# An mLSTM cell followed by hash-routed experts: unread products on TensorE between the two stages, and a shorter hand-over

## The chip, the cores and the metric

The kernel runs on one core of a Trainium2 chip. The metric is the device time of one execution in microseconds (us), taken as the median of several runs. The other numbers come from a profile of one execution: for every engine the instructions with start and duration, and the clock that TensorE was granted over time. The engines are called as in the profile: PE (TensorE, matmuls, with PEld for its weight loads), DVE (VectorE), ACT (ScalarE), POOL (GpSimd) and SP (the queue that issues most transfers).

## The reference, cut to what matters

Two stages follow each other. The first is a recurrent attention cell over 4 batches, 8 heads, 768 steps and heads of 40; its result is laid out as 3072 rows of 320 values. The second sends each row to one of 8 experts by a hash of its token, and each expert is two matrix products with a relu between them.

```python
# stage 1 (per step t): gates, then
C = f_stab * C + i_stab * einsum('bhd,bhe->bhde', vt, kt)
n = f_stab * n + i_stab * kt
h_tilde = einsum('bhde,bhe->bhd', C, qt)
denom = maximum(abs(einsum('bhd,bhd->bh', n, qt)), 1.0)
y[:, :, t] = sigmoid(o_gate[:, :, t]) * h_tilde / denom
# bridge: (B,H,S,D) -> (B*S, H*D)
x = attn_out.transpose(0, 2, 1, 3).reshape(3072, 320)
# stage 2
expert_idx = token_ids * 2654435761 % 8
for e in range(8):
    mask = expert_idx == e
    h = maximum(x[mask] @ w1[e], 0.0)      # 320 -> 1024
    out[mask] = h @ w2[e]                  # 1024 -> 320
```

Everything is fp32 at the inputs and outputs.

## The kernel before

Stage 1 runs over NT = 24 tiles of 128 rows. The last step of each tile, `finish`, divides by the denominator and stores the 128 rows to a scratch array `x_d` in device memory. The two halves of that step are a product on DVE out of PSUM and a product on POOL.

```python
def finish(s):
    ...
    nc.vector.tensor_tensor(den[:], den[:], hs[:, :, :, D:D1], op=ALU.max)
    x = wk.tile([P, H, D], F32, name="x")
    xv = x.rearrange("p (j f) d -> p f j d", f=2)
    nc.vector.tensor_tensor(                                       # L436
        xv, hs[:, :, :, :D], og[s].rearrange(...), op=ALU.mult)
    nc.vector.reciprocal(den[:], den[:])                           # L439
    nc.gpsimd.tensor_tensor(xv, xv, den[:].to_broadcast(...), op=ALU.mult)   # L440
    return lambda: nc.sync.dma_start(x_d[s * P : (s + 1) * P, :], ...)       # L441
```

Stage 2 cannot start before all 24 stores have landed, because an expert's rows may come from any tile. For each expert it gathers NJ = 3 tiles of 128 rows by index, and for each group of EG = 4 experts one further tile with RM = 32 remaining rows of each of them. A gathered tile is turned on PE (three 128x128 transposes into one PSUM tile `tp`) and copied to `xT`, so that an expert works on CAP = 3 * 128 + 32 = 416 columns.

```python
def turn(xg, dst, on_act):
    tp = mps.tile([P, DB, P], F32, name="tp")
    for db in range(2):
        nc.tensor.transpose(tp[:, db, :], xg[:, db * P : (db + 1) * P], ident[:])   # L810
    nc.vector.tensor_copy(xg[:, Dm:], xg[:, 2 * P : Dm])                            # L811
    nc.tensor.transpose(tp[:, 2, :], xg[:, 2 * P :], ident[:])                      # L812
    if on_act:
        nc.scalar.copy(dst, tp[:])                                                  # L814
    else:
        nc.vector.tensor_copy(dst, tp[:])                                           # L816

def turns(e):
    xT = xTs[e] = xp.tile([P, DB, CAP], F32, name="xT")
    def tile_of(j):
        turn(xgs[e][:, j, :], xT[:, :, j * P : (j + 1) * P], j % 2 == 1)
    def remainder():
        i = e % EG
        if i == 0:
            remT[e // EG] = xp.tile([P, DB, P], F32, name="remT")
            turn(xgs[-1 - e // EG], remT[e // EG][:], True)
        nc.gpsimd.tensor_copy(xT[:, :, NM:], remT[e // EG][:, :, i * RM : (i + 1) * RM])   # L896
    return [lambda j=j: tile_of(j) for j in range(NJ)] + [remainder]
```

The driver fetches for two experts, turns the tiles of expert 0, and then goes through the experts. While expert e computes, the tiles of expert e + 1 are turned between its products.

```python
fetch(0)                     # four gathers on POOL: three tiles, then the remainders of four experts
fetch(1)
third = weight_slices(2)
for piece in turns(0):       # the three tiles and the remainder of expert 0
    piece()
for e in range(E):
    ...
    layer1(W[e], xTs[e], h, CAP, one)   # mh[128 x 416] <- w1, xT   (L827, L834)
    ...
    layer2(W[e], h, NJ, ...)            # zp[128 x 320] <- h, w2    (L863)
```

The PSUM tiles of stage 2 come from one pool: `tp` and `zp` with two buffers each, `mh` with four. The weights of experts 0 and 1 are loaded during stage 1.

Of the kernel before, what the change touches and what calls it, by code (L numbers as in the profile page):

```python
# [8 lines left out]
F32 = mybir.dt.float32  # L9
# [5 lines left out]
ALU = mybir.AluOpType  # L15
PSUM = bass.MemoryType.PSUM

P = 128
# [4 lines left out]
def kernel(  # L23
# [24 lines left out]
    nc = tc.nc  # L48
    B, H, S, D = q.shape
# [4 lines left out]
    E, _, F = moe_w1.shape  # L54
    FB = F // P
    NT = N // P
    PR = H // 2
# [9 lines left out]
    RM = 32  # L67
    EG = P // RM
    NM = NJ * P
    CAP = NM + RM  # L70
# [11 lines left out]
    ident = consts.tile([P, P], F32, name="ident")  # L82
# [4 lines left out]
    def weights(src1, src2, wpool, w2pool):  # L87

        w1t = wpool.tile([P, 2, F], F32, name="w1t")
        w1c = wpool.tile([P, FB // 2, P], F32, name="w1c")  # L90
        w2t = w2pool.tile([P, FB, Dm], F32, name="w2t")
        s1 = src1[: 2 * P, :].rearrange("(a p) f -> p a f", p=P)
        last = src1[2 * P :, :].rearrange("d (a two f) -> two d a f", two=2, f=P)
        s2 = src2.rearrange("(a p) d -> p a d", p=P)
        parts = [
            (t[:, db, f0 : f0 + F // 2], s1[:, db, f0 : f0 + F // 2])
            for t in (w1t,) for db in range(2) for f0 in (0, F // 2)
        ]
        parts += [(w1c[i * P // 2 : (i + 1) * P // 2], last[i]) for i in range(2)]
        parts += [(w2t[:, fb : fb + 2, :], s2[:, fb : fb + 2, :]) for fb in range(0, FB, 2)]  # L100
        return (w1t, w1c, w2t), [lambda eng=nc.sync, d=d, r=r: eng.dma_start(d, r) for d, r in parts]

    W = {}

    def weight_slices(e):

        W[e], slices = weights(moe_w1[e], moe_w2[e], wpools[e % 3 // 2], w2pools[2 <= e < 6])
        return slices
# [8 lines left out]
    with tc.tile_pool(name="gates", bufs=1) as gp, \  # L117
# [308 lines left out]
        def finish(s):  # L426
            d = st.pop(s)
            hs = d["xo"].rearrange("p f i (x d) -> p f (i x) d", d=DP)
            den = wk.tile([P, 2, PR, 1], F32, name="den")
            nc.vector.tensor_scalar(  # L430
                den[:], hs[:, :, :, D:D1], scalar1=-1.0, scalar2=1.0, op0=ALU.mult, op1=ALU.max,
# [5 lines that stand above are left out]
                xv, hs[:, :, :, :D], og[s].rearrange("p (j f) d -> p f j d", f=2), op=ALU.mult,  # L437
            )
            nc.vector.reciprocal(den[:], den[:])  # L439
            nc.gpsimd.tensor_tensor(xv, xv, den[:].to_broadcast([P, 2, PR, D]), op=ALU.mult)  # L440
            return lambda: nc.sync.dma_start(x_d[s * P : (s + 1) * P, :], x.rearrange("p h d -> p (h d)"))  # L441


# [343 lines left out]
    mps = ctx.enter_context(tc.tile_pool(name="mps", bufs=2, space=PSUM))  # L787

    def gather(xg, idx):
        nc.gpsimd.indirect_dma_start(  # L790
            out=xg, out_offset=None, in_=x_d[:, :], in_offset=bass.IndirectOffsetOnAxis(ap=idx, axis=0),
        )
# [13 lines left out]
# [8 lines that stand above are left out]
            nc.scalar.copy(dst, tp[:])  # L814
        else:
            nc.vector.tensor_copy(dst, tp[:])  # L816

    def layer1(w, xT, h, cols, between=lambda fp: None):

        w1t, w1c, _ = w  # L820
        for fp in range(FB // 2):
            hp = [mps.tile([P, CAP], F32, name="mh", bufs=4) for _ in range(2)]

            def halves(first):
                for i in range(2):
                    r = slice(i * P // 2, (i + 1) * P // 2)
                    nc.tensor.matmul(  # L827
                        hp[i][:, :cols], lhsT=w1c[r, fp, :], rhs=xT[r, 2, :cols], start=first, stop=not first,
                    )

            def whole(i, first):
                fb = 2 * fp + i
                for db in range(2):
                    nc.tensor.matmul(  # L834
                        hp[i][:, :cols], lhsT=w1t[:, db, fb * P : (fb + 1) * P], rhs=xT[:, db, :cols],
                        start=(first and db == 0), stop=(not first and db == 1),
                    )

            def out(i):
                if i == 0:  # L840
                    nc.vector.tensor_relu(h[:, 2 * fp, :cols], hp[i][:, :cols])  # L841
                else:
                    nc.scalar.activation(h[:, 2 * fp + 1, :cols], hp[i][:, :cols], AF.Relu)  # L843

            if fp % 2 == 0:
                for i in range(2):
                    whole(i, True)
                between(fp)
                halves(False)
                for i in range(2):  # L850
                    out(i)
            else:
                halves(True)
                for i in range(2):
                    whole(i, False)
                    out(i)
                between(fp)
# [15 lines left out]
    with tc.manual_schedule():  # L873
        xgs, xTs, remT, hrem = {}, {}, {}, {}

        def fetch(e):
            if e % EG == 0:
                xgs[-1 - e // EG] = xp.tile([P, DB * P], F32, name="xr")
            xgs[e] = xp.tile([P, NJ, DB * P], F32, name="xg", bufs=3)
            for j in range(NJ):  # L880
                gather(xgs[e][:, j, :Dm], cols_of(g_idx, e * NJ)(j))
            if e % EG == 0:
                gather(xgs[-1 - e // EG][:, :Dm], cols_of(g_idx, NR + e // EG)(0))
# [8 lines that stand above are left out]
                i = e % EG  # L892
                if i == 0:
                    remT[e // EG] = xp.tile([P, DB, P], F32, name="remT")
                    turn(xgs[-1 - e // EG], remT[e // EG][:], True)
                nc.gpsimd.tensor_copy(xT[:, :, NM:], remT[e // EG][:, :, i * RM : (i + 1) * RM])  # L896

            return [lambda j=j: tile_of(j) for j in range(NJ)] + [remainder]

        def rest(g):  # L900
            zp = mps.tile([P, Dm], F32, name="zp")
            for fb in range(FB):
                for i in range(EG):
                    nc.tensor.matmul(
                        zp[i * RM : (i + 1) * RM, :], lhsT=hrem[g][:, i, fb, :], rhs=W[g * EG + i][2][:, fb, :],
                        start=(fb == 0), stop=(fb == FB - 1),
                    )
            scatter(zp, cols_of(s_idx, NR + g)(0), True)

        fetch(0)  # L910
        fetch(1)

        third = weight_slices(2)
        for piece in turns(0):
            piece()
        for e in range(E):
            g, i = e // EG, e % EG
            if e + 2 < E:
                fetch(e + 2)
            h = xp.tile([P, FB, CAP], F32, name="h")  # L920
            if i == 0:
                hrem[g] = xp.tile([P, EG, FB, RM], F32, name="hrem")
            ahead = turns(e + 1) if e + 1 < E else []

            def one(_):
                if ahead:
                    ahead.pop(0)()
                for _ in range(3):
                    if third:
                        third.pop(0)(nc.scalar)  # L930

            def after(j):
                one(j)
                if j == 0 and i == EG - 1:
                    rest(g)

            layer1(W[e], xTs[e], h, CAP, one)
            nc.gpsimd.tensor_copy(hrem[g][:, i], h[:, :, NM:])  # L938
            layer2(W[e], h, NJ, cols_of(s_idx, e * NJ), True, after)
            if e + 3 < E:  # L940
                load_weights(e + 3)

    nx = nc.values_load(xe[0:1, NX : NX + 1], min_val=0, max_val=NX)
    with tc.If(nx > 0):
        with tc.For_i(0, nx, 1) as k:
# [11 lines left out]
            xT = xp.tile([P, DB, CAP], F32, name="xT")  # L957
# [35 lines left out]
```

## Time and profile before

| | before |
|---|---|
| median of 3 runs | 429.63 us (429.09 to 429.99) |
| span of the profiled execution | 427.9 us |
| PE busy | 386.1 us (90% of the span) |
| DVE, ACT, POOL busy | 136.1, 134.6, 118.7 us |
| first transposes of stage 2 start | 173.34 us |
| first expert product starts | 179.17 us |

A row of the profile names the source line, the engine, the operation and its tiles, as output <- inputs. One fp32 matmul of the source appears as two PE records, one fp32 transpose as one. The chain of work is the sequence that ended last, followed back from the end: each piece waited for the one before it. A table of stretches gives for every stretch the busy time of each engine, then PEclk, the clock granted to PE as a share of full speed, and last the share of the transfer engines and their GB/s.

### The profile page before, as it was taken

The page shows a single profiled execution, that of the slowest core. Times are in us where ns is not written, and L with a number is a line of the kernel's source. Part 1 is how long each engine was busy: PE and PEld are TensorE (multiplying, and loading weights), DVE is VectorE, ACT ScalarE, POOL GpSimd, SP SyncE. Part 2 cuts the span into 40 slices and gives each one's busy share as a digit, 9 for nine tenths or more (in the row PEclk, how much of TensorE's full clock was granted, in tenths as well). Part 3 has the DMA queues.
Part 4 walks back from the last instruction along what each step waited for, and adds up shares of the span by engine and source line. Part 5 has one row for each costly group of instructions (what it writes and reads, how often), then busy time and mean ns, then how long its engine had stood idle before and what let it go on. Part 6 is the DMA issues. An engine that isn't in the chain of part 4 may idle for free.

```text
span 427.9 us, 7402 instructions
## 1 busy us (share of the span) xinstructions
PE 386.1 (90%) x2862; PEld 258.5 (60%) x2862; DVE 136.1 (32%) x371; ACT 134.6 (31%) x238; POOL 118.7 (28%) x204
## 2 busy tenths in 40 slices
PE   2369999999999992599999999999999999999992
PEld 2257867877887871356656557556556566575551
DVE  7464748766675761211020120110110210201100
ACT  5158776686495471011010110110111111111010
POOL 6363323313323422710321501302302312021021
PEclk9868999999999998589999999999999999999997
DMA  8929998899676720527616318235216201000000
GB/s 168 213 61 172 206 218 180 190 205 214 149 161 129 161 90 33 163 96 239 193 46 212 120 29 271 62 98 170 75 64 214 61 8 38 0 15 31 1 17 30
DMA packets 111784, 51.37 MB, mean 120 GB/s; under 512 B 86624, under 2 KB 105892, under 8 KB 111748
## 3 DMA queue, kind: packets, MB, share of 16 engines
q1 hardware_dynamic: 105898, 39.31, 38.2%
q0 software_dynamic: 2496, 8.20, 6.0%
q10 hardware_dynamic: 3354, 3.37, 2.4%
q8 instruction: 23, 0.38, 0.4%
q14 instruction: 13, 0.11, 0.1%
HBM read 42.00 MB, written 8.63 MB: 118 GB/s over the span
## 4 chain that ended last, share of the span: by engine, by line
PE 78%; issue 5%; ACT 5%; DMA 4%; POOL 2%; DVE 1%; SPq 1%; ACTq 0%; POOLq 0%; DVEq 0%
PE mh L834 22%; PE zp L863 21%; PE mh L827 6%; PE sp L351 6%; PE ht L409 6%; PE ht L402 3%; PE ab L311 2%; PE tr L275 2%; PE xo L424 2%; PE ht L382 2%; PE tk L588 1%; PE tp L810 1%; ACT qT L289 1%; PE xb L323 1%; PE tr L288 1%
## 5 line engine op out<-in xcount | busy, mean ns | idle before, releaser
L863 PE MATMUL zp<-w2t,h 128*128 128x320 f32 x384 | 105.2, 433 | 0.0
L834 PE MATMUL mh<-xT,w1t 128*128 128x416 f32 x256 | 98.9, 531 | 0.9 <-POOL xT L896 0.9
L863 PEld LDWEIGHTS zp<-w2t,h 128*128 128x128 f32 x384 | 72.7, 190 | 32.1 <-issue 3.3
L834 PEld LDWEIGHTS mh<-xT,w1t 128*128 128x128 f32 x256 | 47.8, 194 | 44.0 <-issue 41.6
L816 DVE COPY xT<-tp 128x384 f32<-128x384 f32 x16 | 8.9, 558 | 142.3 <-PE tp L812 124.7
L797 POOL DMA_INDIRECT out_dram<-zo,s_idx x26 | 25.6, 986 | 92.5 <-ACT zo L796 92.5
L843 ACT ACTIVATE h<-mh 128x416 f32<-128x416 f32 x32 | 16.6, 517 | 110.1 <-PE mh L827 60.3
L796 ACT COPY zo<-zp 128x320 f32<-128x320 f32 x26 | 11.1, 426 | 101.1 <-PE zp L863 92.9
L841 DVE TENSOR_SCALAR h<-mh 128x416 f32<-128x416 f32 x32 | 18.9, 592 | 53.4 <-PE mh L834 26.9
L359 DVE TENSOR_TENSOR w<-sp,w 128x512 f32<-128x512 f32 x48 | 30.9, 686 | 13.8 <-PE sp L351 10.3
L440 POOL TENSOR_TENSOR x<-x,den 128x320 f32<-128x320 f32 x24 | 17.4, 724 | 64.0 <-DVE den L439 34.1
L351 PE MATMUL sp<-qT,kT 64*128 64x128 f32 x384 | 29.7, 297 | 4.1 <-ACT qT L289 4.1
L351 PEld LDWEIGHTS sp<-qT,kT 64*128 64x128 f32 x384 | 24.9, 199 | 10.8 <-ACT qT L289 6.0
L315 ACT ACTIVATE w<-ab 128x512 f32<-128x512 f32 x48 | 26.6, 611 | 5.0 <-PE ab L311 4.9
L409 PE MATMUL ht<-w,v 128*64 128x128 f32 x384 | 27.1, 285 | 0.0
L827 PE MATMUL mh<-xT,w1c 64*128 64x416 f32 x128 | 26.7, 535 | 0.0
L938 POOL COPY hrem<-h 128x256 f32<-128x256 f32 x8 | 3.2, 400 | 84.1 <-ACT h L843 84.1
L790 POOL DMA_INDIRECT xg<-x_rows,g_idx x24 | 23.4, 976 | 9.7 <-issue 9.7
L417 ACT COPY hT<-ht 128x512 f32<-128x512 f32 x24 | 14.1, 587 | 31.2 <-PE ht L409 31.2
L409 PEld LDWEIGHTS ht<-w,v 128*64 128x64 f32 x384 | 21.2, 140 | 4.0 <-issue 3.1
L289 ACT COPY qT<-tr 128x512 f32<-128x512 f32 x24 | 22.9, 975 | 0.6 <-PE tr L288 0.3
L275 PE MATMUL tr<-ident,k 128*128 128x128 f32 x96 | 17.2, 307 | 4.3 <-DMA k<-in_k_dram 4.3
(177 smaller groups left out, 407.0 us busy)
## 6 DMA issues: line engine op xcount, KB each, us to landing
w2t<-in_moe_w_dram SPq DMA_DIRECT2D x28, 320.0 KB
w1t<-in_moe_w_dram SPq DMA_DIRECT2D x28, 256.0 KB
k<-in_k_dram SPq DMA_DIRECT2D x24, 160.0 KB
v<-in_v_dram SPq DMA_DIRECT2D x24, 160.0 KB
og<-in_o_gate_dram SPq DMA_DIRECT2D x24, 160.0 KB
x_rows<-x SPq DMA_DIRECT2D x24, 160.0 KB
ql<-in_q_dram SPq DMA_DIRECT2D x6, 480.0 KB
w1c<-in_moe_w_dram SPq DMA_DIRECT2D x14, 128.0 KB
```

Source lines behind the costliest of these rows:

```text
L275: nc.tensor.transpose(tp[:, j, :], d["k"][:, 2 * j : 2 * j + 2, :].rearrange("p h d -> p (h d)"), ident[:])
L289: nc.scalar.copy(qb[b]["T"][:, :, cols], tp[:])
L315: nc.scalar.activation(w[:, hf], ab[:], AF.Exp)
L351: nc.tensor.matmul(sp[hf][:, j, :], lhsT=d["kT"][r, j, :], rhs=q_of(s)[r, j, :], start=True, stop=True,)
L359: nc.vector.tensor_tensor(d["w"][:, hf], d["sp"][hf][:], d["w"][:, hf], op=ALU.mult)
L409: nc.tensor.matmul(place(j, hf), lhsT=d["v"][:, 2 * j + hf, :], rhs=d["w"][:, hf, j, :], start=(c == 0 and j0 == 0), stop=True, skip_group ...
L790: nc.gpsimd.indirect_dma_start(out=xg, out_offset=None, in_=x_d[:, :], in_offset=bass.IndirectOffsetOnAxis(ap=idx, axis=0),)
L797: ins = nc.gpsimd.indirect_dma_start(out=out[:, :], out_offset=bass.IndirectOffsetOnAxis(ap=idx, axis=0), in_=zo[:], in_offset=None, bound ...
L827: nc.tensor.matmul(hp[i][:, :cols], lhsT=w1c[r, fp, :], rhs=xT[r, 2, :cols], start=first, stop=not first,)
L834: nc.tensor.matmul(hp[i][:, :cols], lhsT=w1t[:, db, fb * P : (fb + 1) * P], rhs=xT[:, db, :cols], start=(first and db == 0), stop=(not fir ...
L841: nc.vector.tensor_relu(h[:, 2 * fp, :cols], hp[i][:, :cols])
L863: nc.tensor.matmul(zp[:], lhsT=h[:, fb, j * P : (j + 1) * P], rhs=w[2][:, fb, :], start=(fb == 0), stop=(fb == FB - 1),)
```

## The change

It has three parts, all at the border of the two stages.

1. TensorE gets products that nobody reads. A PSUM tile `idle` takes one of the four `mh` buffers; `spin(n)` multiplies the identity by 416 columns of the first expert's weights into it. Eleven such products stand between the end of stage 1 and the first transposes of stage 2, and one after each of the four pieces of `turns(0)`. They are there to keep PE active while it would wait for the rows.
2. In the last tile of stage 1 the product with the reciprocal goes from POOL to DVE.
3. The remainder of expert 0 is copied by DVE to `xT` straight from the PSUM tile of its transposes. Before, ACT copied it to `remT` and POOL copied from there. ACT still fills `remT` for the other experts of the group.

```diff
@@ finish
-            nc.gpsimd.tensor_tensor(xv, xv, den[:].to_broadcast([P, 2, PR, D]), op=ALU.mult)
+            eng = nc.vector if s + 1 == NT else nc.gpsimd
+            eng.tensor_tensor(xv, xv, den[:].to_broadcast([P, 2, PR, D]), op=ALU.mult)
@@ turn
             nc.vector.tensor_copy(dst, tp[:])
+        return tp
@@ remainder
                     remT[e // EG] = xp.tile([P, DB, P], F32, name="remT")
-                    turn(xgs[-1 - e // EG], remT[e // EG][:], True)
+                    tp = turn(xgs[-1 - e // EG], remT[e // EG][:], True)
+                if e == 0:
+                    nc.vector.tensor_copy(xT[:, :, NM:], tp[:, :, :RM])
+                    return
                 nc.gpsimd.tensor_copy(xT[:, :, NM:], remT[e // EG][:, :, i * RM : (i + 1) * RM])
@@ driver
         third = weight_slices(2)
+        idle = mps.tile([P, CAP], F32, name="mh", bufs=4)
+        def spin(n):
+            for _ in range(n):
+                nc.tensor.matmul(idle[:], lhsT=ident[:], rhs=W[0][0][:, 0, :CAP], start=True, stop=True)
+        spin(11)
         for piece in turns(0):
             piece()
+            spin(1)
```

Apart from this, the order of the instructions on every engine is the same. In the built program the first product of the eleven waits for the product L436 of the last tile, which reads the PSUM that its output takes over. The new DVE copy of the remainder waits for the ACT copy out of the same PSUM tile.

## The prediction, made before the changed kernel was run

> **What bounds the kernel now.** I read the page first. PE is busy for 386.1 of 427.9 us, so a gain must come from the few slices (of 10.7 us) in which it isn't:
>
> ```profile
> PE   2369999999999992599999999999999999999992
> ...
> PEclk9868999999999998589999999999999999999997
> ```
>
> PE's digits fall to 2 and 5 in slices 16 and 17, about 160 to 182 us; the clock falls with them, to 8, 5 and 8. That is the border of the two stages. Behind it PE stays at 9 to the end, and no wait of PE for weights is listed, so I take a microsecond won at the border to arrive at the end whole.
>
> Next, the chain of work from the last store of stage 1 to the first experts (start, duration, what):
>
> ```profile
> 166.50 0.73 POOL x L440
> ...
> 167.24 1.77 DMA x_rows<-x
> ...
> 170.02 1.19 POOL xg L790
> 171.21 0.30 issue
> 171.51 0.95 POOL xg L790
> 172.46 0.30 issue
> 172.77 0.95 POOL xg L790
> 173.72 0.30 issue
> 174.02 3.24 DMA xr<-x_rows,g_idx
> 177.26 0.14 issue
> 177.40 0.66 PE tp L810 x2
> 178.06 0.23 PE tp L812
> 178.28 0.02 issue
> 178.31 0.49 ACT remT L814
> 178.79 0.06 issue
> 178.85 0.27 POOL xT L896
> 179.12 0.04 issue
> 179.17 5.74 PE mh L834 x8
> ```
>
> The border is a row of waits: the POOL product, the store, four gathers at 1.25 us each, the landing of the fourth (the remainders) at 177.26, its transposes, two copies. PE has only the transposes in it. The last line is the second thing to see: 8 records in 5.74 us, 718 ns each. The same 8 records in the second expert (at 210.78 of the same chain) take 2.79 us, 349 ns each. The table of stretches says why (duration, then busy PE, PEld, DVE, ACT, POOL; then PEclk):
>
> ```profile
> 164.20:167.60 3.40, 0.66 (x4) 0.42 (x4) 0.84 (x4) 0.17 (x1) 0.72 (x1) 0.99 0.14 51
> 167.60:171.00 3.40, 0.00 (x0) 0.00 (x0) 0.00 (x0) 0.00 (x0) 0.98 (x1) 0.50 0.14 48
> ...
> 177.80:181.20 3.40, 2.50 (x6) 1.25 (x5) 0.20 (x1) 0.48 (x1) 2.81 (x4) 0.50 0.64 197
> 181.20:184.60 3.40, 3.40 (x6) 1.58 (x5) 0.00 (x0) 0.00 (x0) 1.53 (x3) 0.50 0.76 275
> 184.60:188.00 3.40, 3.40 (x16) 1.70 (x15) 1.15 (x2) 0.52 (x1) 0.00 (x0) 1.00 0.00 0
> ```
>
> PE's last work of stage 1 ends at 165.08; the clock halves at 167.6 and comes back only at 184.6, 5.4 us after the first product at 179.17.
>
> **What the Trainium skill says.** (1) "TensorE: Matmul & The Clock Gate", "Part 1: The HAM clock gate": the clock is halved after an idle window and released after a busy one; the window is 3.4 us and free-running. The trace agrees: I cut the table in steps of 3.4 us back from the fall. The window with 0.66 us of PE work ends in the fall, the first one full of work (3.40) ends in the rise, one with 2.50 doesn't raise it. (2) The same page, "Why this matters for your kernels": no gaps of PE over about 3 us. The gap here is 8.3 us, from 165.08 to 173.34. (3) "GPSIMD Engine Reference", "Engine selection": a two-input elementwise operation belongs on VectorE, GpSimd taking about twice as long. Here L440 takes 0.72 us on POOL and L436, of the same 128x320 on DVE, 0.49: a ratio of 1.5. (4) "PSUM — Partial Sum Buffer", Terms: two engines must not touch a bank at once, reads included. That explains why the new DVE copy waits for ACT's copy of the same tile in the built program, and takes most of the worth out of part 3.
>
> **Part 2: the product on DVE.** L439 ends on DVE at 166.06 (165.87 + 0.19); POOL starts L440 at 166.50 and ends at 167.23. On DVE it can follow at 166.1 and, at L436's 0.49, ends at 166.6. The store, all gathers and all landings come 0.65 us earlier: the remainders at 177.26 - 0.65 = 176.6, the first tile (whose transposes start on landing at 173.34) at 172.7.
>
> **Part 1: the eleven products.** Each is a 128x416 fp32 product like L834: two records of 349 ns, 0.70 us at the full clock. The first waits for L436, which ends at 165.95, so they run from about 166.1 to 166.1 + 11 * 0.70 = 173.8. The first tile has landed at 172.7: the products overrun it by 1.1 us. From there PE, and no longer the gathers, paces the four pieces. At the full clock three transposes between products cost 0.33 us (0.22 + 0.11 in the chain at 189.82), and each piece is followed by a product of 0.70: 1.03 per piece. The pieces start at 173.8, 174.8, 175.9 and 176.9. Landings, one per 1.25 us, would have allowed 172.7, 173.9, 175.1 and 176.6. So the overrun shrinks from 1.1 to 0.3 us by the last piece, and I add 0.1 to 0.2 because DVE copies the first tile (0.56) and then the narrow columns of the second (0.2) before its third transpose can go.
>
> **Part 3 and the start of the experts.** The last transposes end at about 177.5 instead of 178.29. Then ACT's copy runs (0.49, unchanged), then the new DVE copy, which I put at 0.2 (the 64-column copy L811 takes 0.20, POOL's L896 0.27), with 0.1 for two hand-overs: 178.35. The product behind the last piece ends at about 178.1 and doesn't delay this. Expert 0 starts at 178.35 instead of 179.17: 0.8 us won. Only 0.07 of this is the direct copy; about 0.65 is the DVE product, 0.4 the transposes at the full clock, less the overrun of 0.3 to 0.5.
>
> **The clock.** The window that lost the clock held 0.66 us of PE work; with products from 166.1 to 167.6 it holds 2.2 of 3.4. A window with that share kept it: from 160.8 to 164.2, PE is busy for 2.3 us and nothing falls. From 173.8 on, pieces and products leave PE almost no gap. So expert 0 starts at the full clock: its first 8 records take 2.79 for 5.74 (2.95 won), and the transposes behind them are about as long as before.
>
> **Sum.** 0.8 + 2.95 = 3.75 us. Afterwards nothing moves: PE is full and waits for no weights; the gathers of expert 1 start 0.65 earlier too, and its first transposes, now at about 181.1, need a gather that was issued at 175.28 and will be issued at 174.6. At the measured 3.2 from issue to landing that is 177.9. Weights of the third expert are issued by ACT in the same place of its order, 0.8 us earlier, and are needed 60 us later. 429.63 - 3.75 = 425.9 us, a ratio of 0.991.
>
> **Rivals.** *The overrun costs more.* If each piece loses a few hand-overs (a wait of PE on DVE for the third transpose, about 0.1 to 0.25 in the records at 174.5), the last piece starts up to 0.8 late and the expert's start is not won at all: 0 + 2.95, time 426.7. For it: PE is in order, and a product in front of a piece that is ready can't be passed. *The products hide completely.* If they start earlier or run shorter, the landings pace the pieces and the start is won by 1.1 to 1.2: time 425.4. Against it: L436 releases the first one, and 349 ns is seen on 256 records. *The clock falls all the same.* The window is free-running; if one ends so that it holds the waits at 163.7 to 164.4 and 165.1 to 166.1 together, its share is about half, and I don't know on which side of the threshold that is (0.22 of a window falls, 0.67 doesn't). Then the eleven products run at half speed, 1.4 us each, until the next full window releases them, some 3.4 us: about 1.7 us lost in the overrun, the clock still back by 175. Time 427.5. *The half clock costs less on average than in this profile.* The rise comes at a window's end, so in other executions it would come 3.4 to 6.8 us after the start and cost 1.7 to 3.4. The three times before lie within 0.9 us and the profiled one, 429.59, is their middle, so 2.95 is not far off; but it could be 2.5, time 426.3. *A new bound behind the border*, weights or gathers: nothing speaks for it, the last loads of weights finish long before the end.
>
> **Range and chances.** The middle of these is 425.9. The low end, 425.1, is both terms at their best with the scatter of 0.4 of the runs. The high end, 427.2, is the overrun at its worst and the clock's term at its lower value. Faster by over 2% would need 8.6 us, which is about the whole gap of PE; slower by over 2% would need the half clock to last through stage 2. So 0.97 for within 2%.
>
> **What would show it.** Right: PEclk at 9 in slices 16 to 18; L834's first 8 records at about 2.8 us; the product with the reciprocal as a DVE row of 0.4 to 0.5 us, and the store 0.65 earlier; eleven products of 0.70 that begin 0.1 after L436 ends; the first transposes start when the eleven end, not when rows land; expert 0 starts at 178.0 to 178.7. Wrong: any product of 1.4 us; landings that are not earlier; a first start later than 179.2; or a gap of PE for weights behind the border.

## The result and the profile after

The changed kernel takes 426.12 us (median of 4 runs, 425.5 to 426.55) against 429.69 us: a ratio of 0.9918, with a 95% interval of 0.9900 to 0.9935. Predicted were 425.9 us, with a range of 425.1 to 427.2.

The page of the changed kernel, its rows of PE and of the granted clock in 40 slices:

```profile
PE   2369999999999997999999999999999999999992
...
PEclk9988999999999999999999999999999999999998
```

The dip of PE in slices 16 and 17 is filled but for a 7, and the clock's digits 8, 5, 8 have become 9, 9, 9. The chain of work through the border has another shape (start, duration, what):

```profile
164.99 0.12 DVE den L439
165.11 0.03 issue
165.14 7.92 PE mh L924 x22
173.06 0.22 PE tp L811 x2
173.27 0.11 PE tp L813
173.38 0.70 PE mh L924 x2
...
176.19 0.22 PE tp L811 x2
176.41 0.16 PE tp L813
176.57 0.70 PE mh L924 x2
177.27 0.48 issue
177.75 3.06 PE mh L836 x8
```

Before, the chain went through the POOL product, the store and the gathers. Now, from the last steps of stage 1 on DVE, it goes through PE: the unread products themselves (L924) carry it from the end of stage 1 to the first expert. In the timeline one sees the product on DVE, the first gather, and how the last piece is handed over, which the chain only calls "issue":

```profile
165.13 0.49 DVE L441 TENSOR_TENSOR x<-x,den 128x320 f32<-128x320 f32 x1
...
168.42 1.19 POOL L791 DMA_INDIRECT xg<-x_rows,g_idx  x1 [5.55 <-issue]
...
176.25 0.33 PE L813 MATMUL tp<-ident,xr 128*128 128x128 f32 x1
...
176.93 0.48 ACT L815 COPY remT<-tp 128x384 f32<-128x384 f32 x1 [1.83 <-PE tp L813]
...
177.44 0.26 DVE L899 COPY xT<-tp 128x96 f32<-128x96 f32 x1 [1.25 <-ACT remT L815]
```

ACT starts 0.36 us after the transposes end (176.57), where before it started 0.03 after them; DVE waits for ACT.

To compare kernels I use two lengths of a profile, because they don't depend on where stage 1 ended in that execution. The **border** runs from the start of L430 of the last tile (the first step on its denominator) to the first product of expert 0. The **first block** runs from there through 8 records and three transposes to the first product of the 64-row weights (L827, L829 after the change). Before: 13.98 and 6.06, together 20.04 us. Changed: 13.52 and 3.39, together 16.91. So the border and the first block give 3.13 us. The rest of the two spans is equal (242.67 and 242.66 us from there to the end), and the profile's remaining 0.96 us of difference lies ahead of L430, where nothing was changed. Nearly all of it arises around 100 us, where PE waits for a transfer of stage 1 (`R<-decay_pieces`, L311), 0.27 and 0.28 us long before and not at all in the changed kernel's profile: from the twelfth L430 to the fourteenth it is 12.10 us before and 11.18 after.

### The profile page after: what moved, and what is told of

Its sections match the earlier page's. It is cut to its first block, busy times and chain, and to the rows that moved or that the text cites. A ratio compares the mean times of both kernels' runs of the same rounds, so it can differ in the third digit from the quotient of the medians.

```text
span 423.8 us, 7461 instructions
## 1 busy us (share of the span) xinstructions
PE 392.1 (93%) x2892; PEld 262.1 (62%) x2892; DVE 136.2 (32%) x373; ACT 134.3 (32%) x238; POOL 117.7 (28%) x202
## 4 chain that ended last, share of the span: by engine, by line
PE 84%; ACT 5%; issue 5%; POOL 2%; DVE 1%; ACTq 1%; DMA 1%; POOLq 0%; DVEq 0%
PE mh L836 22%; PE zp L865 21%; PE sp L351 7%; PE ht L409 6%; PE mh L829 6%; PE ht L402 3%; PE mh L924 3%; PE ab L311 2%; PE tr L275 2%; PE xo L424 2%; PE ht L382 2%; PE tr L288 2%; PE tk L589 2%; PE tp L811 1%; PE xb L323 1%
## 5 line engine op out<-in xcount | busy, mean ns | idle before, releaser
L836 PE MATMUL mh<-xT,w1t 128*128 128x416 f32 x256 | 96.2, 519 | 0.5 <-issue 0.5
L836 PEld LDWEIGHTS mh<-xT,w1t 128*128 128x128 f32 x256 | 46.7, 190 | 42.7 <-issue 41.6
L829 PE MATMUL mh<-xT,w1c 64*128 64x416 f32 x128 | 26.7, 535 | 0.0
L275 PE MATMUL tr<-ident,k 128*128 128x128 f32 x96 | 17.4, 309 | 4.1 <-POOL R L638 4.1
```

Of the source, the lines that this page charges most:

```text
L275: nc.tensor.transpose(tp[:, j, :], d["k"][:, 2 * j : 2 * j + 2, :].rearrange("p h d -> p (h d)"), ident[:])
L829: nc.tensor.matmul(hp[i][:, :cols], lhsT=w1c[r, fp, :], rhs=xT[r, 2, :cols], start=first, stop=not first,)
L836: nc.tensor.matmul(hp[i][:, :cols], lhsT=w1t[:, db, fb * P : (fb + 1) * P], rhs=xT[:, db, :cols], start=(first and db == 0), stop=(not fir ...
```

## The experiments

The clock column says whether it was halved at the border in the profiled execution.

| kernel | time, us | ratio to before, 95% interval | border | first block | sum | clock at the border |
|---|---|---|---|---|---|---|
| before | 429.69 | 1 | 13.98 | 6.06 | 20.04 | half for 17.1 us |
| changed | 426.12 | 0.9918 (0.9900 to 0.9935) | 13.52 | 3.39 | 16.91 | full |
| changed_again | 426.18 | 0.9948 (0.9914 to 0.9982) | 15.02 | 3.39 | 18.41 | half for 3.4 us |
| spins_only | 428.91 | 0.9977 (0.9960 to 0.9993) | 15.67 | 3.39 | 19.06 | half for 3.4 us |
| no_spins | 429.30 | 0.9980 (0.9966 to 0.9995) | 13.25 | 6.28 | 19.53 | half for 17.1 us |
| no_last | 427.90 | 0.9946 (0.9926 to 0.9966) | 13.55 | 3.39 | 16.94 | full |
| spins14 | 431.79 | 1.0024 (0.9992 to 1.0057) | 19.30 | 4.84 | 24.14 | half twice, 3.4 us each |
| gapfree | 426.03 | 0.9930 (0.9908 to 0.9951) | 13.21 | 3.39 | 16.60 | full |
| spins9 | 425.74 | 0.9919 (0.9890 to 0.9947) | 12.99 | 3.39 | 16.38 | full |
| no_between | 427.58 | 0.9967 (0.9953 to 0.9981) | 14.33 | 3.38 | 17.71 | half for 3.4 us |
| narrow_first | 427.26 | 0.9941 (0.9915 to 0.9967) | 13.05 | 3.38 | 16.43 | full |
| border_best | 425.94 | 0.9921 (0.9890 to 0.9951) | 12.68 | 3.38 | 16.06 | full |
| border_and_early | 431.30 | 1.0042 (1.0023 to 1.0062) | 12.60 | 3.39 | 15.99 | full |
| early_mended | 425.02 | 0.9878 (0.9855 to 0.9902) | 12.54 | 3.38 | 15.92 | full |

Times of different rows come partly from different chips, on which the kernel before took 429.25 to 430.07 us; the ratios take that out. They come from all times of both kernels and are not quite the quotient of the two medians. All edits below are against the changed kernel; the last two kernels have those of border_best as well.

**spins_only**: the unread products alone.

```diff
-            eng = nc.vector if s + 1 == NT else nc.gpsimd
+            eng = nc.gpsimd
-                if e == 0:
-                    nc.vector.tensor_copy(xT[:, :, NM:], tp[:, :, :RM])
-                    return
```

> Part 1 alone: the unread products stay, the product with the reciprocal is back on POOL, the remainder is copied by ACT and POOL again. Border means from the start of the last tile's L430 to the start of the first expert product: 13.98 us before, 13.52 in the changed kernel; first block means from there to the start of L827/L829: 6.06 before, 3.39 changed. If the clock carries the gain (my theory): no half clock, first block 3.4, border 13.9 to 14.2 because landings are 0.65 later but PE is less overrun; time 426.3 to 427.0. If the shorter hand-over carries it (rival): most of the gain is gone, time above 428.5.

Measured: 428.91 us. The first block is 3.39, as the clock theory has it, but the border is 15.67, over a microsecond longer than either side expected: the eleven products took 9.62 us and not 7.9. The clock had halved inside them, at 167.8, for one window. So the first block is the clock theory's, but the time is the rival's (above 428.5): alone, the unread products are worth 0.2% (interval 0.07 to 0.40%), about a quarter of what the change brought. The possibility that the prediction had among its rivals, "the clock falls all the same", had come in; and ACT took the remainder over only 0.75 us after its transposes ended.

**no_spins**: parts 2 and 3 alone.

```diff
-        spin(11)
         for piece in turns(0):
             piece()
-            spin(1)
```

> Parts 2 and 3 alone, no unread products. Clock theory: the clock halves in the gap again, first block 5.0 to 6.1, border 13.98 - 0.65 - 0.07 = about 13.3; time about 429.0. Hand-over theory: time below 427.

Measured: 429.30 us, border 13.25 against 13.3 expected, and the clock half for 17.1 us, as before. Without the unread products the change is worth 0.2% (interval 0.05 to 0.34%). The hand-over theory, with its time below 427, falls: the shorter border is real (0.73 us), but it is not the gain. By the times, then, neither half brings the gain alone; each has about a quarter of it.

**changed_again**: the changed kernel once more.

> The changed kernel itself, once more, because in the runs so far the clock fell for 3.4 us inside the eleven products of one profile (part 1 alone) and did not fall in two others, with the same two waits of PE ahead of them. Theory: whether it falls depends on where the free-running window ends, so the times of the changed kernel come in two groups, some 1.7 to 2.5 us apart, with the lower one at 425.5 to 426.5 and the median between them, 426 to 428. Rival: the clock holds in the changed kernel always; one group, within 1 us.

Measured: 426.18 us; the six times are 425.90, 425.96, 426.13, 426.23, 427.49 and 429.25. The profiled execution is the one of 427.49, and in it the clock halves at 165.86. The stretches of this profile, cut at the clock's windows of 3.41 us (busy PE first, PEclk third from the end):

```profile
159.04:162.45 3.41, 2.67 (x50) 2.02 (x44) 1.71 (x6) 0.58 (x1) 0.00 (x0) 1.00 0.11 37
162.45:165.86 3.41, 1.65 (x21) 1.20 (x16) 1.13 (x6) 0.58 (x1) 0.72 (x1) 1.00 0.14 50
165.86:169.28 3.42, 3.42 (x6) 1.65 (x6) 0.27 (x1) 0.00 (x0) 0.35 (x1) 0.50 0.13 48
169.28:172.69 3.41, 3.41 (x11) 1.82 (x11) 0.28 (x1) 0.00 (x0) 2.74 (x3) 1.00 0.34 95
```

And those of the changed kernel's first profile, whose windows end elsewhere:

```profile
161.20:164.61 3.41, 2.17 (x36) 1.52 (x32) 1.13 (x7) 0.59 (x1) 0.72 (x1) 1.00 0.14 50
164.61:168.02 3.41, 2.88 (x9) 1.64 (x10) 0.98 (x3) 0.00 (x0) 0.00 (x0) 1.00 0.14 48
168.02:171.44 3.42, 3.42 (x11) 1.89 (x10) 0.00 (x0) 0.00 (x0) 2.41 (x3) 1.00 0.16 48
```

Same program, same waits of PE: 0.74 us for ACT's copy and 1.02 us ahead of the first unread product. In the first profile a window's end at 164.61 parts them; the two windows hold 2.17 and 2.88 us of work, and nothing happens. In the second both fall into one window, which holds 1.65 of 3.41, and at its end the clock halves for exactly one window, in which only 6 records start instead of 11. The border is 1.5 us longer for it. Of eight profiles with unread products and these two waits left open, four show this fall (changed_again, spins_only, spins14, no_between). An estimate from the first profile agrees: from the start of the first wait to the end of the second it is 2.4 us (162.7 to 165.14), so a window of 3.41 holds both whole in about 0.3 of its possible positions, and holds less than 0.60 of work in about half of them. With the fall, border and first block save 20.04 - 18.41 = 1.63 us, not much more than spins_only (0.98) and no_spins (0.51) together; the step to 3.13 is the fall that the first profile was spared.

**gapfree**: two more unread products in PE's waits of the last two tiles and one ahead of the eleven, written to a score tile's PSUM, which is free by then.

```diff
+                if s == NT - 1:
+                    fill(1)
                 back(s - 1)
...
+        fill(1)
         back(NT - 1)
+        fill(1)
         finish(NT - 1)()
```

These are three products in all, not the four that the expectation speaks of.

> The changed kernel with four more unread products, three of them in PE's waits of 0.74 us for ACT in the last two tiles of stage 1 and one ahead of the eleven; they write a score tile's PSUM, which is free by then, and so wait for nothing late. Theory (a window's share of work decides): the clock can't fall at the border in any execution, the upper group is gone, median at 425.5 to 426.5 on a chip where the kernel before takes 430. Rival (the spread comes from elsewhere): the spread is that of the changed kernel.

Measured: 426.03 us, 424.98 to 427.14, at 0.9930, and no fall at the border. The windows of this profile:

```profile
160.41:163.82 3.41, 3.41 (x43) 2.29 (x40) 0.85 (x4) 0.73 (x2) 0.72 (x1) 1.00 0.00 0
163.82:167.24 3.42, 3.10 (x12) 1.49 (x11) 1.33 (x5) 0.44 (x1) 0.00 (x0) 1.00 0.14 50
```

The least share is now 0.91, and no stretch of 3.41 us around these waits holds less in this profile, wherever it begins. In none of the four kernels with these fills did the clock fall at the border. By the times alone the case isn't settled: the intervals of gapfree and changed_again overlap, and a spread of 2.2 us remains, which I expected to be smaller.

**spins9**: nine products for eleven.

```diff
-        spin(11)
+        spin(9)
```

> 9 products in place of 11. If PE overruns the landings by 1.1 us at the first tile, 9 end 0.3 us ahead of its landing and the landings pace the pieces: border 13.0 to 13.3 instead of 13.52, time 0.2 to 0.5 below the changed kernel in executions with a full clock. If the overrun costs nothing by the last piece (rival): border 13.5.

Measured: border 12.99, at the edge of 13.0 to 13.3, and 425.74 us. The chain has gone back to the gathers:

```profile
171.82 0.95 POOL xg L791
172.76 0.30 issue
173.07 3.27 DMA xr<-x_rows,g_idx
176.34 0.14 issue
176.48 0.41 PE tp L811 x2
176.88 0.12 PE tp L813
177.01 0.02 issue
177.03 0.49 ACT remT L815
177.52 0.02 issue
177.54 0.27 DVE xT L899
```

Transposes start 0.14 after the landing: PE is no longer late. The overrun of the eleven products did cost time, but less than 13.52 - 12.99: some 0.3 us of that is the late hand-over to ACT, which this profile doesn't have. Against gapfree, whose eleven products end as late and whose hand-over is prompt too (border 13.21), nine are worth 0.22 us. In the times the two can't be told apart.

**spins14**: fourteen for eleven.

```diff
-        spin(11)
+        spin(14)
```

> 14 products in place of 11 ahead of the first tile. If PE is already overrun, as the trace of the changed kernel has it, each further product is on the path: border 13.52 + 3 * 0.70 = 15.6, time 2.1 us above the changed kernel, about 428.2. If the products hide in the wait for the gathers (rival), border below 14.2 and time within 0.7 us of the changed kernel.

Measured: border 19.30, not 15.6, and 431.79 us, above the kernel before or equal to it (1.0024, 0.9992 to 1.0057). The direction and the rule (each further product is on the path) are right. The size has two more terms. The fall inside the products costs some 1.7 us, and the signals of PE come late: DVE begins the third tile's copy 0.57 us after its transposes end, and ACT the remainder's 1.8 us after. In that wait PE does little, and the clock halves again:

```profile
181.88:185.29 3.41, 1.57 (x6) 0.50 (x4) 0.66 (x2) 0.38 (x1) 0.94 (x1) 1.00 0.38 105
185.29:188.71 3.42, 2.97 (x5) 1.54 (x6) 0.36 (x2) 0.10 (x1) 0.26 (x1) 0.50 0.73 218
```

**no_last**: no product behind the remainder's transposes.

```diff
-        for piece in turns(0):
+        for n, piece in enumerate(turns(0)):
             piece()
-            spin(1)
+            if n < 3:
+                spin(1)
```

> The changed kernel without the one unread product behind the remainder's transposes. There, ACT's copy of the remainder starts 0.36 us after the transposes end, against 0.04 in the kernel before and 0.04 to 0.16 for the other tiles. If the product behind delays the signal of the transposes: ACT starts within 0.1 us, border 13.52 - 0.3 = 13.2. If the delay is of another origin: border 13.5 as before. In both cases the full clock stays; time 425.8 to 426.2.

Measured: border 13.55, and ACT starts 0.38 after the transposes end (179.11 and 179.49), as in the changed kernel. The product behind is not the cause of the late signal. Where PE was full ahead of it, the same hand-over takes 0.02 to 0.04 in two profiles from one chip (changed_again, gapfree) and 0.36 to 1.8 in five others (changed, spins_only, no_last, spins14, narrow_first). Whether the chip makes the difference isn't shown, and since the ends of PE's records are modelled, it isn't shown either that the signal, and not the record, is off. The time expected, 425.8 to 426.2, is missed (427.90), with times from 425.87 to 430.60.

**no_between**: no products between the pieces.

```diff
         for piece in turns(0):
             piece()
-            spin(1)
```

> Eleven products ahead of the first tile, none after the four pieces. If the products between are needed for the clock: PE is busy for about 0.33 of 1.25 us for nearly 4 us, the clock falls in most executions and the first block takes 4.5 to 6, time 1.5 to 3 us above the changed kernel. If the eleven are enough: first block 3.4 and the border 13.2, time 0.3 below.

Measured: 427.58 us. In the profile the clock falls inside the eleven products (a window with a share of 0.48, as above) and not later: while the pieces run, the windows hold 0.81 and 0.64 of PE work, and that is enough. So the products between the pieces weren't needed in this execution, and the expected fall in the first block didn't come (3.38). Another position of the windows should bring it, since from 176.44 on 3.41 us of this profile hold only 0.45 of PE work; this is an estimate, no run shows it. The time lies 1.4 us above changed_again and doesn't separate the two falls.

**narrow_first**: DVE's narrow copy ahead of ACT's.

```diff
-                    tp = turn(xgs[-1 - e // EG], remT[e // EG][:], True)
-                if e == 0:
-                    nc.vector.tensor_copy(xT[:, :, NM:], tp[:, :, :RM])
+                    turn(xgs[-1 - e // EG], remT[e // EG][:], True,
+                         (lambda tp: nc.vector.tensor_copy(xT[:, :, NM:], tp[:, :, :RM])) if e == 0 else None)
+                if e == 0:
                     return
@@ turn, ahead of its copy
+        if first:
+            first(tp)
         if on_act:
```

> The changed kernel with the two copies out of the remainder's PSUM tile in the other order: DVE takes its 96 columns first, ACT fills remT after it. In the changed kernel ACT's 0.49 us stand on the path ahead of DVE's 0.27. If that wait is what part 3 lost: the border falls by up to 0.5, to about 13.0, where the product behind the last piece (0.70) becomes the limit; time 0.3 to 0.5 below the changed kernel at equal clock. If the copies are not on the path: border unchanged.

Measured: border 13.05, 0.47 less than the changed kernel, with the product behind the last piece as the new limit. The copy straight from PSUM brings most in this order. The time, 427.26 at 0.9941, doesn't show it: stage 1 ended at 166.5 in this profile and at 164.2 in that of the changed kernel, and such differences are larger than the effect.

**border_best**: nine products, the fills of gapfree, DVE first, none behind the last piece.

> Everything that the runs point to at the border: 9 products, the four that fill PE's waits ahead of them, DVE's copy first, no product behind the last piece. Expected border 12.5 to 12.7 (the landing of the remainders 11.5 after L430, transposes 0.67, copy 0.3), first block 3.4, no fall of the clock at the border; time about 425.0 to 425.5 and a spread of at most 1.5 us, from stage 1 alone. If the fills cost more than they save: no lower than 425.7.

Measured: border 12.68, first block 3.38, no fall, as expected; 425.94 us at 0.9921. The sum of 16.06 is 0.85 below the changed kernel's. The time is above what was expected and not to be told from that of spins9; the spread of 2.5 us is wider than expected.

**border_and_early**: border_best with twelve further products in the first 29 us of stage 1, where PE waits for the gates.

```diff
+        warm(4)
         gates_turn(g0)
+        warm(3)
         decays(0)
...
             state(s)
+            if s == 0:
+                warm(5, st[0]["ht"])
```

> The kernel border_best with twelve further unread products in the three waits of PE in the first 29 us of stage 1 (4, 3 and 5 of them), where every profile so far has the clock at half for 3.4 to 10 us. If the rest of the spread comes from there: one group of times within 0.6 us, 1 to 2.5 us below border_best, about 423.5. If PE's products there delay the gates (they stand in order ahead of transposes and decays that may be ready): no gain or a loss of up to 2 us.

Measured: 431.30 us, worse than before (1.0042). The last five wrote the tile that DVE's copy of the state reads, so they waited for DVE and held up PE:

```profile
23.61 0.79 PE L382 MATMUL ht<-v,kw 128*64 128x41 f32 x16
30.70 6.03 PE L672 MATMUL ht<-k,ident 128*128 128x416 f32 x10 [6.30 <-DVE C L386]
36.66 0.41 PE L323 MATMUL xb<-R,Lx 128*64 128x512 bf16 x2
```

The products that follow them started at 28.78 in the kernel before and at 36.66 here. An unread product is work in order, with waits of its own.

**early_mended**: the same, the five written to a score tile's PSUM.

```diff
-                warm(5, st[0]["ht"])
+                warm(5, ps.tile([P, PR, P], F32, name="sp0").rearrange("p j t -> p (j t)"))
```

> The twelve products of border_and_early again, but the last five write a score tile's PSUM, which DVE has read by 25.6 us, instead of the tile that waited for DVE's copy of the state (that wait put them at 30.7 and cost some 5 us). If the rest of the spread and of the half clock comes from stage 1: no stretch at half clock but the one at the end, one group of times within 0.8 us, 1 to 2.5 us below border_best, a ratio to the kernel before of 0.986 to 0.990. If they stand in the way again, or the chain there is not PE's: within 0.5 us of border_best or above.

Measured: 425.02 us at 0.9878 (0.9855 to 0.9902), the lowest ratio of all and in the range expected, though its interval touches those of spins9 and border_best. The five run at full clock in the wait that they are meant for:

```profile
25.12 3.76 PE L673 MATMUL sp<-k,ident 128*128 128x416 f32 x10 [0.65 <-DVE w L359]
28.87 0.41 PE L323 MATMUL xb<-R,Lx 128*64 128x512 bf16 x2
29.21 1.16 PE L351 MATMUL sp<-qT,kT 64*128 64x128 f32 x16
```

In the kernel before, the scores after this wait took 2.08 us for the same 16 records, at half clock. The expected single group within 0.8 us did not come: the times run from 423.51 to 426.93, and in the profiled one the clock still halves once, at 36.35. So these products didn't narrow the spread, and how much of it is stage 1's clock isn't shown. (PEclk reads full ahead of a profile's first clock record, but PE wasn't: in the kernel before, the four transposes L275 take 1.12 us at 11.82 and 0.66 once the clock is full.) Another part can be seen in the profiles: the times between the L430 of successive tiles agree within 0.1 us over most tiles, but from the twelfth to the fourteenth they add up to 11.18 us in the changed kernel's profile and to 13.05 in that of no_last, which waits 1.29 us there in one piece for `R<-decay_pieces`.

## Why the prediction was right

**The clock** (predicted 2.95 us) is most of the gain in a profile without a fall, and its size was nearly right: 6.06 - 3.39 = 2.67 us. The missing 0.28 is the start of the row of products. I took 2.79 for 8 records, the value between other products; after PE's wait of 0.48 they take 3.06. That no fall happens at the border is true of the first profile, and half of the profiles with the same waits show the rival that I priced at 427.5 us: "the clock falls all the same". changed_again has it at 427.49. That the first four times met 425.9 so closely is thus in part luck: measured again, the same kernel gave 0.9948, 2.2 us of gain in place of 3.5. The open place in the prediction was the share of a window on which it turns, which I knew only to lie between 0.22 (my table has 0.66 of 3.40, which is 0.19) and 0.67. The profiles put it between 0.48 (falls) and 0.60 (doesn't).

**The product on DVE** was right: it starts 0.03 after the reciprocal's end and takes 0.49, gathers start 0.64 earlier counted from L430 (168.42 - 164.23 against 170.02 - 165.19), and the remainders land 0.67 earlier (11.40 after L430 against 12.07).

**The eleven products** were right: 7.92 us from 0.15 after L436, the end overruns the landing of the first tile (171.61) by 1.4 us, and by the last piece 0.40 is left (175.63 and 176.03) where I had 0.3 to 0.5. spins9 against gapfree puts the cost of this overrun at 0.22 us of border.

**Part 3 and the start of the experts** was the term that was off: 0.8 us predicted, 13.98 - 13.52 = 0.46 measured. Counted from L430, the transposes of the remainder ended where I had them (12.34; predicted 177.5 - 165.19 = 12.31). Behind them I had 0.1 for two hand-overs and 0.2 for DVE's copy; ACT's hand-over alone took 0.36 and the copy 0.26. The late hand-over is not the fault of the product behind (no_last). Its cause stays open.

**The sum**: 3.75 predicted, 3.13 shown in border and first block, 3.57 in the medians (429.69 - 426.12). The 0.44 between the last two is not explained by the change: stage 1 ended between 164.2 and 167.3 us in all profiles of this study but that of border_and_early, and with a few runs such differences don't average out. changed_again gives 0.9948 with an interval that overlaps the first. The waits for `R<-decay_pieces` around 100 us are one part of this spread, the clock in the first 36 us perhaps another; how much of the 0.44 is due to either is open.

Of the other rivals, *the overrun costs more* did not come in: the remainder's transposes ended where I had them, and the 0.34 us that are missing at the border were lost behind them. *The half clock costs less on average* was not tested; the two profiles without unread products have first blocks of 6.06 and 6.28 us, so they show no smaller cost. *The products hide completely* falls with spins9 and spins14, and *a new bound behind the border* with the equal 242.7 us.

## What to carry to other kernels

Where PE waits long enough to lose its clock ahead of dense products, unread products in the wait buy the clock back: in the profiles the first block took 3.4 us with the full clock and 6.1 to 6.3 without. Don't expect them to do it alone; by the times, products alone and hand-over alone brought about 0.2% each, and both together 0.5 to 0.8%. Count the products against the earliest landing and rather stop early (nine were better at the border than eleven, fourteen gave everything back), give them PSUM that is free at once, and fill the short waits ahead of them too, because a window adds them up. Then look at what hands the last data over: the order of two copies out of one PSUM tile was worth as much at the border (0.47 us) as the change had won there (0.46 us), one profile each.

## What the runs showed of the hardware that I had not expected

- The Trainium skill, "TensorE: Matmul & The Clock Gate", section "Part 1: The HAM clock gate", speaks of an idle window. The profiles show that the window need not be idle: at the border the clock fell behind windows in which PE's records fill 0.19 (twice), 0.46 (once) and 0.48 (four times), in stage 1 behind 0.46 in early_mended and 0.42 in border_and_early. It stayed full behind 0.60 (once each in no_between, narrow_first and border_best), 0.64 or more.
- For the rise the share alone doesn't decide. At the border the clock rose behind 0.87 (spins14) and 1.00, and not behind 0.66, 0.73, 0.74 or 0.75; but in stage 1 it stayed at half behind 0.80 (changed), 0.87 (spins9) and 0.89 (spins14). What else counts isn't shown.
- A fall in the middle of dense products lasted one window, 3.41 us, in four profiles, and cost about half of it: the eleven products took 9.6 instead of 7.9 us.
- After dense products ACT or DVE began up to 0.75 us after PE's record had ended (1.8 once, with fourteen products), in five profiles and not in two others. The product behind the last piece is not the cause (no_last); the cause is open.
